# Opening an attention-and-FFN kernel by pairs of heads and 256 tokens, with tanh in the first gelus and a new column order

## The chip, the cores and the metric

One core of one Trainium2 chip. The metric is the device time of one execution, in microseconds (us). Engines: PE (matmul), PEld (weight load, overlapping PE), DVE (VectorE), ACT (ScalarE), POOL (GpSimd, which issues most loads here), SP (SyncE).

## The reference

```python
k_proj = einsum('ks,bhsd->bhkd', E, k);  v_proj = einsum('ks,bhsd->bhkd', F, v)   # 8 x 8 heads, 1024 tokens, D = 64, 64 projected keys
attn = softmax(q @ k_proj^T / 8);  x = attn @ v_proj       # x becomes [8192 tokens, 512]
h = x @ w_in;  g = h * sigmoid(1.702 * h)                  # w_in [512, 2048]
return g @ w_out                                           # float32 [8192, 512]
```

## The kernel before

The 8192 tokens go through in 16 blocks of 512. For each block, `ffn1` makes 16 columns of 128 hidden units (four matmuls and a gelu), `ffn2` multiplies by w_out, and attention work for later blocks is put between the matmuls by `at(block, slot, ...)`. Only block 0 has no earlier block to hide in: its attention stands in the open, and its first FFN runs in two halves of 256 tokens. The parts concerned:

```python
load_kv(k, kt, 0, "k_sb", H // 2)            # two loads
load_kv(q, qt, 0, "q0_sb", H, 0, JB)         # q's first half
load_kv(v, vt, 0, "v_sb", H // 2)            # two loads
for i in range(3): load_w_in(i)              # w_in in 8 pieces of 2 columns each
load_kv(q, qt, 0, "q0_sb", H, JB, JB)        # q's second half
for i in range(3, 8): load_w_in(i)
...
ps_f = ...tile_pool(name="ps_f", bufs=4, space=PSUM)   # one ring of four for k, v, q, scores, ffn1, ffn2, warm-ups
...
for g in range(2):
    k_half(proj0(0, g), g); warm(3)          # warm(n): n matmuls on zeros
for g in (0, 1): q_tr(0, g)()                # q transposed; g = 1 is copied by ScalarE
warm(4)
for u in range(2): scores(0, u)()            # four exps of 512
gelu_table()
for g in range(2):
    v_part(0, proj0(1, g), slice(g, g + 1)); warm(2)
tok(0, 0)(); tok(0, 1)()                     # 128 tokens, all heads: attn @ v, reciprocal, multiply
x_tr(0, 0)(); x_tr(0, 1)()                   # transposes and one 512-wide copy into xT
at(0, 0, tok(0, 2)); at(0, 1, tok(0, 3)); at(0, 4, x_tr(0, 2)); at(0, 6, x_tr(0, 3))
...
for i in range(halves * FC):                 # block 0: half 0's 16 columns, then half 1's
    hf, fc = divmod(i, FC)
    ffn1(j, fc, ...); filled(j, i)
```

The softmax here doesn't subtract the row's maximum and nothing guards it: scores larger than these inputs give would overflow.

## Time and profile before

| | before |
|---|---|
| three executions first seen | 521.7, 521.79, 523.04 us |
| the profiled one | 521.73 us, span 520.0 us |
| first FFN matmul / block 1's first FFN matmul in the chain | 23.79 / 58.44 us |
| PE's granted clock, 23.4 to 26.6 us | 0.50 |

The chain of waits is followed backwards from the last instruction, so it shows what the end hung on. The lines of each view are in the prediction.

### The profile page before, as it was taken

What the parts mean: (1) busy time and instruction counts of PE and PEld (TensorE: products, weight loads), DVE (VectorE), ACT (ScalarE), POOL (GpSimd) and SP (SyncE); (2) the same over time, 40 slices, a digit from 0 to 9 for tenths busy, and PEclk for the clock granted to TensorE, in tenths of its full rate; (3) what the DMA queues carried; (4) which work ended last, traced back from release to release, by engine and by line L of the source; (5) the groups of instructions that cost most, each with busy time, mean ns of one, the idle gap of its engine ahead of it and who ended that gap; (6) DMA issues with size and microseconds to landing.
All of it is one profiled execution on the core that took longest, in us unless ns stands there. A gap on an engine that the chain in (4) does not pass through costs nothing.

```text
span 520.0 us, 6643 instructions
## 1 busy us (share of the span) xinstructions
PE 509.9 (98%) x2830; PEld 233.1 (45%) x2830; DVE 246.6 (47%) x210; ACT 264.4 (51%) x433; POOL 75.7 (15%) x94
## 2 busy tenths in 40 slices
PE   7799999999999999999999999999999999999996
PEld 3485544443444444444444444444444444444442
DVE  2321323674865480827648183664808265560000
ACT  1466355464546547364555645465473646344351
POOL 6354320921510015000420000000000000000000
PEclk9899999999999999999999999999999999999999
DMA  9999999999996019760494301060200101010102
GB/s 169 200 203 185 236 186 160 167 186 156 225 167 162 1 81 153 95 163 0 123 178 119 72 12 76 2 161 2 82 5 1 81 1 81 1 81 2 81 1 81
DMA packets 112750, 53.78 MB, mean 103 GB/s; under 512 B 85584, under 2 KB 110160, under 8 KB 110800
## 3 DMA queue, kind: packets, MB, share of 16 engines
q0 software_dynamic: 83328, 29.37, 49.8%
q1 hardware_dynamic: 29312, 23.73, 16.3%
q8 instruction: 22, 0.36, 0.3%
q10 hardware_dynamic: 80, 0.26, 0.2%
q14 instruction: 8, 0.07, 0.0%
HBM read 59.24 MB, written 16.78 MB: 146 GB/s over the span
## 4 chain that ended last, share of the span: by engine, by line
PE 96%; ACT 1%; DMA 1%; DVE 1%; issue 0%; ACTq 0%
PE f_ps L304 43%; PE f_ps L293 43%; PE f_ps L140 2%; PE f_ps L218 2%; PE d_ps L218 1%; PE n_ps L218 1%; DMA ef_f<-in_E_dram 1%; PE d_ps L264 1%; PE n_ps L279 1%; ACT expT L230 1%; PE f_ps L119 0%; PE f_ps L197 0%; PE f_ps L149 0%; PE f_ps L200 0%; DVE x_sb L270 0%; ACT L234 0%
## 5 line engine op out<-in xcount | busy, mean ns | idle before, releaser
L250 DVE RECIPROCAL rden<-d_ps 128x512 f32<-128x512 f32 x52 | 174.3, 3352 | 149.3 <-PE d_ps L218 149.3
L304 PE MATMUL f_ps<-w_out_sb,gT 128*128 128x512 bf16 x1024 | 230.6, 379 | 0.1
L293 PE MATMUL f_ps<-xT,w_in_sb 128*128 128x512 bf16 (+1 forms) x1088 | 228.4, 368 | 0.7 <-DVE xT L281 0.6
L295 ACT ACTIVATE gT<-f_ps 128x512 bf16<-128x512 f32 (+1 forms) x272 | 155.5, 572 | 89.0 <-PE f_ps L293 87.7
L293 PEld LDWEIGHTS <-w_in_sb 128*128 128x128 bf16 x1088 | 105.4, 98 | 116.9 <-issue 4.9
L304 PEld LDWEIGHTS <-gT 128*128 128x128 bf16 x1024 | 97.2, 98 | 122.4 <-issue 11.3
L307 ACT COPY o_sb<-f_ps 128x512 f32<-128x512 f32 x64 | 37.5, 586 | 138.3 <-PE f_ps L304 128.5
L63 POOL DMA_DIRECT2D q_sb<-in_q_dram x56 | 49.1, 895 | 67.4 <-DMA k_sb<-in_k_dram 28.9
L251 DVE TENSOR_TENSOR xT<-n_ps,rden 128x512 bf16<-128x512 f32 x52 | 36.0, 692 | 5.8 <-DVE rden L250 0.5
L230 ACT ACTIVATE expT<-f_ps 128x512 bf16<-128x512 f32 x64 | 34.8, 600 | 4.7 <-PE f_ps L218 4.7
L57 POOL DMA_DIRECT2D k_sb<-in_k_dram x9 | 7.8, 862 | 107.6 <-PE f_ps L140 105.9
L230 ACT ACT_TABLE_LOAD x13 | 16.7, 1283 | 4.7 <-PE f_ps L218 4.5
L234 ACT ACT_TABLE_LOAD x14 | 18.0, 1283 | 0.2
L269 DVE RECIPROCAL rd<-d_ps 128x4 f32<-128x4 f32 x24 | 4.2, 174 | 22.6 <-PE d_ps L264 22.5
L140 PE MATMUL f_ps<-k_sb,eft 128*64 128x512 bf16 x56 | 13.4, 382 | 0.0
L140 PE MATMUL f_ps<-v_sb,eft 128*64 128x512 bf16 x56 | 13.4, 382 | 0.0
L218 PE MATMUL f_ps<-qT,kt 64*64 64x512 bf16 x128 | 13.2, 399 | 0.1
L204 DVE COPY qT<-f_ps 128x1024 bf16<-128x1024 bf16 x7 | 4.8, 691 | 16.3 <-PE f_ps L200 8.8
L119 PE MATMUL f_ps<-zeros 128*128 128x512 bf16 x30 | 10.1, 480 | 1.2 <-DVE zeros L101 1.2
L270 DVE TENSOR_TENSOR x_sb<-d_ps,rd 128x256 bf16<-128x256 f32 x24 | 10.2, 424 | 0.8
L218 PE MATMUL d_ps<-expT,ones 64*64 64x512 bf16 x104 | 10.2, 382 | 0.0
L218 PE MATMUL n_ps<-expT,vq 64*64 64x512 bf16 x104 | 10.0, 376 | 0.0
(47 smaller groups left out, 99.1 us busy)
## 6 DMA issues: line engine op xcount, KB each, us to landing
out_dram<-o_sb SPq DMA_DIRECT2D x15, 1024.0 KB, 4.5
k_sb<-in_k_dram POOLq DMA_DIRECT2D x7, 1024.0 KB, 15.9
q_sb<-in_q_dram POOLq DMA_DIRECT2D x56, 128.0 KB, 11.3
v_sb<-in_v_dram POOLq DMA_DIRECT2D x7, 1024.0 KB, 10.5
w_in_sb<-in_moe_w_in_dram POOLq DMA_DIRECT2D x8, 256.0 KB, 14.4
w_out_sb<-in_moe_w_out_dram POOLq DMA_DIRECT2D x4, 512.0 KB, 14.1
k_sb<-in_k_dram POOLq DMA_DIRECT2D x2, 512.0 KB, 7.5
q_sb<-in_q_dram POOLq DMA_DIRECT2D x2, 512.0 KB, 13.8
```

The costliest lines, as they stand in the source:

```text
L63: nc.gpsimd.dma_start(out=qt[b][:, j], in_=qv[:, j])
L140: nc.tensor.matmul(kvps[b][r], eft[:, j, e * KP:(e + 1) * KP], (kt, vt)[e][b][:, :, j, :], start=(j == 0), stop=(j == J - 1))
L218: nc.tensor.matmul(outs[i][r], lhsTs[i][ri], rhss[i][ri], start=True, stop=True)
L230: nc.scalar.activation(expT[h][:, 2 * u + i, :], s_ps[i], AF.Exp, scale=scale)
L234: nc.scalar.preload_act_table(AF.Gelu_apprx_sigmoid)
L250: nc.vector.reciprocal(rden, d_ps[i])
L251: nc.vector.tensor_tensor(x_of(h)[:, 2 * u + i, :], n_ps[i], rden, op=ALU.mult)
L270: nc.vector.tensor_tensor(xs[h, t][:, 4 * g:4 * g + 4, :], d_ps[:, :, :D], rd.to_broadcast([P, 4, D]), op=ALU.mult)
L293: nc.tensor.matmul(h_ps, w_in_sb[:, kc, fc * P:(fc + 1) * P], xT[j][:, kc, ts], start=(kc == 0), stop=(kc == KC - 1))
L295: nc.scalar.activation(gts[j][:, fc, ts], h_ps, AF.Gelu_apprx_sigmoid)
L304: nc.tensor.matmul(o_ps[0], gts[j][:, fc, n * P:(n + 1) * P], w_out_sb[:, fc, :], start=(fc == 0), stop=(fc == FC - 1))
L307: nc.scalar.copy(osb[j][:, n, :], o_ps[0])
```

## The change

Its intent: start the FFN earlier by doing only what the first 256 tokens need. q's first quarter is loaded and transposed, the scores and exps are 256 wide, and tok and x_tr go by pairs of heads, so that v's last heads can come later, in small loads. The second 256 tokens' exps come after the FFN has begun. So that they need no switch of ScalarE's table, the first five gelus are made from tanh and two DVE steps. The first FFN's order is changed too: twelve columns for each half, then four. The diff, cut to its core:

```diff
+    load_kv(q, qt, 0, "q0_sb", H, 0, 2)
+    load_kv(v, vt, 0, "v_sb", ((0, 4), (4, 2), (6, 2)))
+    load_kv(q, qt, 0, "q0_sb", H, 2, 2)
+    for i in range(6): load_w_in(i)          # was: 3 pieces, q's second half, 5 pieces
 ...
-            cp = nc.scalar.copy if b == 0 and g == 1 else nc.vector.tensor_copy
-            cp(qT[b][:, 2 * g:2 * g + 2], t_ps)
+            nc.vector.tensor_copy(qT[b][:, 2 * g:2 * g + 2], t_ps)
 ... # v_out: one 64x64 copy per head, ScalarE and DVE in turn (was: two copies of two heads)
 ... # tok(h, p, half), x_tr(h, p, half): a pair of heads and 256 tokens (was: 128 tokens, all heads)
+        if j > 0 or ts.start > 0 or fc > 4:
+            nc.scalar.activation(gts[j][:, fc, ts], h_ps, AF.Gelu_apprx_sigmoid)
+        else:
+            t_sb = work.tile([P, n], F32, name="t_sb", bufs=3)
+            nc.scalar.activation(t_sb, h_ps, AF.Tanh, scale=0.851)
+            nc.vector.tensor_scalar(t_sb, t_sb, 0.5, 0.5, op0=ALU.mult, op1=ALU.add)
+            nc.vector.tensor_tensor(gts[j][:, fc, ts], t_sb, h_ps, op=ALU.mult)
 ...
+    q_tr(0, 0)(); warm(3); scores(0, 0, 0)(); scores(0, 1, 0)()
+    v_out(0, proj0(1, 0, 4), 0, 2); warm(2)
+    tok(0, 0, 0)(); tok(0, 1, 0)(); v_out(0, proj0(1, 4, 2), 2, 1)
+    x_tr(0, 0, 0)(); x_tr(0, 1, 0)(); tok(0, 2, 0)(); v_out(0, proj0(1, 6, 2), 3, 1)
+    x_tr(0, 2, 0)(); tok(0, 3, 0)(); q_tr(0, 1)(); x_tr(0, 3, 0)()
+    order = [(half, fc) for fcs in (range(12), range(12, FC)) for half in range(2) for fc in fcs]
+    at(0, 0, scores(0, 0, 1)); at(0, 1, scores(0, 1, 1)); at(0, 4, gelu_table)
+    for p in range(HP):
+        at(0, 5 + p, tok(0, p, 1)); at(0, 8 + p, x_tr(0, p, 1))
 ... # block 1: load(1) takes v ahead of q, proj(1) four slots earlier; block 0's first FFN2 parts swapped
```

More of the change, by code (lines that the diff above doesn't have):

```diff
@@ L55, in load_kv @@
         sv = src[b].rearrange("h (p j) d -> p h j d", p=P)
-        for h in range(0, H, hs):
-            nc.gpsimd.dma_start(out=dst[b][:, h:h + hs, js:js + jn], in_=sv[:, h:h + hs, js:js + jn])
+        for h, n in [(h, hs) for h in range(0, H, hs)] if isinstance(hs, int) else hs:
+            nc.gpsimd.dma_start(out=dst[b][:, h:h + n, js:js + jn], in_=sv[:, h:h + n, js:js + jn])
     def load_q(b):
@@ L66, in load @@
         load_kv(k, kt, b, "k_sb")
+        if b == 1:
+            load_kv(v, vt, b, "v_sb")
         load_q(b)
-        load_kv(v, vt, b, "v_sb")
+        if b > 1:
+            load_kv(v, vt, b, "v_sb")
     w_in_v = moe_w_in.rearrange("(c p) f -> p c f", p=P)
@@ L81 @@
     make_identity(nc, ident)
-    load_kv(q, qt, 0, "q0_sb", H, 0, JB)
-    load_kv(v, vt, 0, "v_sb", H // 2)
-    for i in range(3):
+    load_kv(q, qt, 0, "q0_sb", H, 0, 2)
+    load_kv(v, vt, 0, "v_sb", ((0, 4), (4, 2), (6, 2)))
+    load_kv(q, qt, 0, "q0_sb", H, 2, 2)
+    for i in range(6):
         load_w_in(i)
     load_kv(q, qt, 0, "q0_sb", H, JB, JB)
-    for i in range(3, 8):
+    for i in range(6, 8):
         load_w_in(i)
@@ L143, in proj, with proj0 @@
         return go
-    def proj0(e, g):
-        ps = f_tile([P, H // 2, D])
-        hs = slice(g * H // 2, (g + 1) * H // 2)
+    def proj0(e, h0, n):
+        ps = f_tile([P, n, D])
         for j in range(J):
-            nc.tensor.matmul(ps, eft[:, j, :], (kt, vt)[e][0][:, hs, j, :],
+            nc.tensor.matmul(ps, eft[:, j, :], (kt, vt)[e][0][:, h0:h0 + n, j, :],
                              start=(j == 0), stop=(j == J - 1))
@@ L164, in k_tr, with v_out @@
         nc.vector.tensor_copy(kts[b % 2][:, p0:p0 + n, :], t_ps)
-    def v_part(b, v_ps, us):
-        vv = v_ps[HI].rearrange("k (u x) d -> k u x d", x=4)
-        for r, xs_, n in ((LO, X_LO, 0), (HI, X_HI, 1)):
-            if b < 2:
-                cp = nc.scalar.copy if b == 0 and n else nc.vector.tensor_copy
-                cp(vxs[b][r].rearrange("k (u x) d -> k u x d", x=4)[:, us, xs_, :D], vv[:, :, xs_, :])
-            if b > 0:
-                nc.vector.tensor_copy(vqs[b % 2][r].rearrange("k (u e) d -> k u e d", e=2)[:, us],
-                                      vv[:, :, xs_, :])
+    def v_out(b, v_ps, p0, n):
+        for i in range(n):
+            p = p0 + i
+            for r, t in ((LO, p % 2), (HI, 1 - p % 2)):
+                if b < 2:
+                    cp = nc.scalar.copy if b == 0 and t == p % 2 else nc.vector.tensor_copy
+                    cp(vxs[b][r, 2 * p + t, :D], v_ps[HI, 2 * i + t, :])
+        if b > 0:
+            vv = v_ps[HI].rearrange("k (u x) d -> k u x d", x=4)
+            for r, xs_ in ((LO, X_LO), (HI, X_HI)):
+                nc.vector.tensor_copy(vqs[b % 2][r].rearrange("k (u e) d -> k u e d", e=2), vv[:, :, xs_, :])
     def kv_out(b):
@@ L182, in go @@
                 nc.sync.dma_start_transpose(out=kts[b % 2], in_=k_b.rearrange("k h d -> k (h d)"))
-            v_part(b, ps, slice(0, 2))
+            v_out(b, ps, 0, HP)
             kbs[b] = k_b
@@ L218, in four, with scores @@
                 nc.tensor.matmul(outs[i][r], lhsTs[i][ri], rhss[i][ri], start=True, stop=True)
-    def scores(h, u):
+    def scores(h, u, half=None):
         b, c = divmod(h, NB2)
+        j0, n = (c * JB, JB) if half is None else (c * JB + half * JB // 2, JB // 2)
+        ts = slice(j0 * P - c * TB, (j0 + n) * P - c * TB)
         def go():
-            if u == 0:
+            if h not in expT:
                 expT[h] = att.tile([P, HP, TB], BF16, name="expT", bufs=3)
-            s_ps = [f_tile([P, TB]) for _ in range(2)]
+            s_ps = [f_tile([P, n * P]) for _ in range(2)]
             four(s_ps, [kts[b % 2][:, 2 * u + i, :] for i in range(2)],
-                 [qT[b][:, c * JB:(c + 1) * JB, 2 * u + i, :] for i in range(2)])
+                 [qT[b][:, j0:j0 + n, 2 * u + i, :] for i in range(2)])
             for i in range(2):
-                nc.scalar.activation(expT[h][:, 2 * u + i, :], s_ps[i], AF.Exp, scale=scale)
+                nc.scalar.activation(expT[h][:, 2 * u + i, ts], s_ps[i], AF.Exp, scale=scale)
         return go
@@ L255, with tok @@
     xs = {}
-    def tok(h, t):
+    def tok(h, p, half):
         def go():
-            xs[h, t] = work.tile([P, H, D], BF16, name="x_sb")
-            for g in range(2):
-                d_ps = ps_d.tile([P, 4, D + 1], F32, name="d_ps")
-                for i in range(2):
-                    p = 2 * g + i
-                    nc.tensor.matmul(d_ps[:, 2 * i:2 * i + 2, :].rearrange("s t d -> s (t d)"),
-                                     expT[h][:, p, t * P:(t + 1) * P],
-                                     vxs[h // NB2][:, 2 * p:2 * p + 2].rearrange("r t d -> r (t d)"),
-                                     start=True, stop=True)
-                rd = work.tile([P, 4, 1], F32, name="rd")
-                nc.vector.reciprocal(rd, d_ps[:, :, D:])
-                nc.vector.tensor_tensor(xs[h, t][:, 4 * g:4 * g + 4, :], d_ps[:, :, :D],
-                                        rd.to_broadcast([P, 4, D]), op=ALU.mult)
+            d_ps = ps_d.tile([P, 4, D + 1], F32, name="d_ps")
+            for i in range(2):
+                t = 2 * half + i
+                nc.tensor.matmul(d_ps[:, 2 * i:2 * i + 2, :].rearrange("s t d -> s (t d)"),
+                                 expT[h][:, p, t * P:(t + 1) * P],
+                                 vxs[h // NB2][:, 2 * p:2 * p + 2].rearrange("r t d -> r (t d)"),
+                                 start=True, stop=True)
+            rd = work.tile([P, 4, 1], F32, name="rd")
+            nc.vector.reciprocal(rd, d_ps[:, :, D:])
+            xs[h, p, half] = work.tile([P, 4, D], BF16, name="x_sb", bufs=4)
+            nc.vector.tensor_tensor(xs[h, p, half], d_ps[:, :, :D], rd.to_broadcast([P, 4, D]), op=ALU.mult)
@@ L272, in tok, with x_tr @@
         return go
-    def x_tr(h, t):
+    def x_tr(h, p, half):
         def go():
-            x_sb = xs.pop((h, t)).rearrange("s h d -> s (h d)")
-            n_ps = ps_n.tile([P, KC, P], BF16, name="n_ps")
-            for c in range(KC):
-                nc.tensor.transpose(n_ps[:, c, :], x_sb[:, c * P:(c + 1) * P], ident)
-            cp = nc.scalar.copy if (h, t) == (0, 0) else nc.vector.tensor_copy
-            cp(x_of(h)[:, :, t * P:(t + 1) * P], n_ps)
+            x_sb = xs.pop((h, p, half)).rearrange("s (i t) d -> s i (t d)", i=2)
+            n_ps = ps_n.tile([P, 2, P], BF16, name="n_ps")
+            for i in range(2):
+                nc.tensor.transpose(n_ps[:, i, :], x_sb[:, i, :], ident)
+            nc.vector.tensor_copy(x_of(h)[:, p, half * TB // 2:(half + 1) * TB // 2],
+                                  n_ps.rearrange("r i s -> r (i s)"))
@@ L294, in ffn1, with ffn2 @@
                              start=(kc == 0), stop=(kc == KC - 1))
-        nc.scalar.activation(gts[j][:, fc, ts], h_ps, AF.Gelu_apprx_sigmoid)
-    def ffn2(j, n, half):
-        b, c = divmod(j, S // TB)
-        if n == 0 and half == 0:
+        if j > 0 or ts.start > 0 or fc > 4:
[5 more added lines that the diff above has]
+            nc.vector.tensor_tensor(gts[j][:, fc, ts], t_sb, h_ps, op=ALU.mult)
+    def ffn2(j, n, fcs):
+        b, c = divmod(j, NB2)
+        if j not in osb:
             osb[j] = work.tile([P, JB, DM], F32, name="o_sb")
-        if half == 0:
-            o_ps[0] = f_tile([P, DM])
-        for fc in range(half * FC // 2, (half + 1) * FC // 2):
-            nc.tensor.matmul(o_ps[0], gts[j][:, fc, n * P:(n + 1) * P], w_out_sb[:, fc, :],
+        if fcs.start == 0:
+            o_ps[n] = f_tile([P, DM])
+        for fc in fcs:
+            nc.tensor.matmul(o_ps[n], gts[j][:, fc, n * P:(n + 1) * P], w_out_sb[:, fc, :],
                              start=(fc == 0), stop=(fc == FC - 1))
-        if half == 1:
-            nc.scalar.copy(osb[j][:, n, :], o_ps[0])
+        if fcs.stop == FC:
+            nc.scalar.copy(osb[j][:, n, :], o_ps.pop(n))
             ov = out[b * S:(b + 1) * S, :].rearrange("(p j) m -> p j m", j=J)
@@ L321 @@
     for g in range(2):
-        k_half(proj0(0, g), g)
+        k_half(proj0(0, 4 * g, 4), g)
         warm(3)
-    for g in (0, 1):
-        q_tr(0, g)()
-    warm(4)
+    q_tr(0, 0)()
+    warm(3)
     for u in range(2):
-        scores(0, u)()
-    gelu_table()
-    for g in range(2):
-        v_part(0, proj0(1, g), slice(g, g + 1))
-        warm(2)
-    tok(0, 0)()
-    tok(0, 1)()
-    x_tr(0, 0)()
-    x_tr(0, 1)()
-    at(0, 0, tok(0, 2))
-    at(0, 1, tok(0, 3))
-    at(0, 4, x_tr(0, 2))
-    at(0, 6, x_tr(0, 3))
-    at(0, 18, q_tr(0, 2))
-    at(0, 20, q_tr(0, 3))
-    at(0, Q, scores(1, 0))
-    at(0, Q + 1, scores(1, 1), gelu_table)
-    for t in range(JB):
-        at(0, Q + 2 + t, tok(1, t))
-        at(0, Q + 3 + t, x_tr(1, t))
+        scores(0, u, 0)()
+    v_out(0, proj0(1, 0, 4), 0, 2)
+    warm(2)
+    tok(0, 0, 0)()
+    tok(0, 1, 0)()
+    v_out(0, proj0(1, 4, 2), 2, 1)
+    x_tr(0, 0, 0)()
+    x_tr(0, 1, 0)()
+    tok(0, 2, 0)()
+    v_out(0, proj0(1, 6, 2), 3, 1)
+    x_tr(0, 2, 0)()
+    tok(0, 3, 0)()
+    q_tr(0, 1)()
+    x_tr(0, 3, 0)()
+    order = [(half, fc) for fcs in (range(12), range(12, FC)) for half in range(2) for fc in fcs]
+    at(0, 0, scores(0, 0, 1))
+    at(0, 1, scores(0, 1, 1))
+    for p in range(HP):
+        at(0, 5 + p, tok(0, p, 1))
+        at(0, 8 + p, x_tr(0, p, 1))
+    at(0, 20, q_tr(0, 2))
+    at(0, 23, q_tr(0, 3))
+    at(0, 4, gelu_table)
+    for u in range(2):
+        at(0, Q + u, scores(1, u))
+    at(0, Q + 1, gelu_table)
+    for p in range(HP):
+        at(0, Q + 2 + p, tok(1, p, 0), tok(1, p, 1))
+        at(0, Q + 3 + p, x_tr(1, p, 0), x_tr(1, p, 1))
+    at(1, 4, proj(1))
+    at(1, 5, kv_out(1))
+    at(1, 7, lambda: k_tr(1, kbs[1], 0), q_dma(2))
     for g in range(4):
-        at(1, 2 + 2 * g, q_tr(1, g))
-    at(1, 8, proj(1))
-    at(1, 9, kv_out(1))
-    at(1, 10, lambda: k_tr(1, kbs[1], 0), q_dma(2))
+        at(1, 8 + 2 * g, q_tr(1, g))
     for u in range(2):
@@ L357 @@
         at(2, O + 3 + u, scores(5, u))
-    for t in range(JB):
-        at(1, O + 2 + t, tok(2, t))
-        at(1, O + 3 + t, x_tr(2, t))
+    for p in range(HP):
+        at(1, O + 2 + p, tok(2, p, 0), tok(2, p, 1))
+        at(1, O + 3 + p, x_tr(2, p, 0), x_tr(2, p, 1))
     at(2, 1, norm(3, 0))
@@ L387 @@
             load(j // NB2 + 2)
-        halves = 2 if j == 0 else 1
-        for i in range(halves * FC):
-            hf, fc = divmod(i, FC)
-            ffn1(j, fc, slice(hf * TB // halves, (hf + 1) * TB // halves))
+        for i, (half, fc) in enumerate(order if j == 0 else [(None, fc) for fc in range(FC)]):
+            ffn1(j, fc, slice(0, TB) if half is None else slice(half * TB // 2, (half + 1) * TB // 2))
             filled(j, i)
-        for s in range(2 * JB):
-            ffn2(j, s // 2, s % 2)
-            filled(j, halves * FC + s)
+        parts = [(n, range(8 * g, 8 * g + 8)) for n in range(JB) for g in range(2)]
+        if j == 0:
+            parts[1:3] = parts[2:0:-1]
+        for s, (n, fcs) in enumerate(parts):
+            ffn2(j, n, fcs)
+            filled(j, (Q if j == 0 else O) + s)
     assert not fill, fill
```

## The prediction

> **What bounds the kernel now.** I read first the busy table of the whole execution, to see which engine has no room:
>
> ```profile
> span 520.0 us, 6643 instructions
> PE 509.9 (98%) x2830; PEld 233.1 (45%) x2830; DVE 246.6 (47%) x210; ACT 264.4 (51%) x433; POOL 75.7 (15%) x94
> ...
> PE   7799999999999999999999999999999999999996
> ...
> PEclk9899999999999999999999999999999999999999
> ```
>
> PE is full everywhere but in the first two slices (13 us each) and the last. "Busy" is not "at its peak", so next the stretch sums, which give pace as well:
>
> ```profile
> core 0: us, PE busy (x) PEld busy (x) DVE busy (x) ACT busy (x) POOL busy (x), PEclk, DMA share, GB/s
> 19.90:23.40 3.50, 1.88 (x17) 0.93 (x15) 2.33 (x9) 1.02 (x4) 1.49 (x3) 0.99 1.45 194
> 23.40:26.60 3.20, 2.81 (x17) 2.01 (x18) 1.59 (x7) 0.77 (x2) 1.24 (x2) 0.50 1.45 196
> ...
> 29.42:41.90 12.48, 12.44 (x133) 10.43 (x132) 1.81 (x3) 9.39 (x25) 5.42 (x7) 1.00 1.27 205
> ```
>
> PE has half its time free from 19.9 to 23.4, and in the 3.2 us after that its granted clock is 0.50. From 29.4 on it is full at clock 1.00. In the chain that ended last, eight 512-column matmuls take 1.73 us piece after piece, 0.216 us each; 64 of them, one half of a block's FFN, are 13.8 us. From 93.7 us on, PE is busy 416.2 of 416.3 us. The diff takes no matmul out of that part, so it can only move the opening: when the first FFN matmul starts (23.79 us), and how long block 0 then takes (block 1 starts at 58.44, so 34.65 us).
>
> The same chain shows what holds the start back:
>
> ```profile
> 13.99 1.03 PE f_ps L197 x32
> ...
> 15.04 1.02 ACT qT L204
> ...
> 16.11 0.46 PE f_ps L218 x4
> 16.57 2.04 ACT expT L230 x4
> ...
> 18.63 1.28 ACT L234
> ...
> 19.93 0.27 ACT vx L171
> ...
> 22.41 0.44 DVE x_sb L270
> ...
> 23.22 0.43 DVE xT L281
> ...
> 23.79 1.01 PE f_ps L293 x4
> ```
>
> q is transposed and ScalarE copies the second half (1.02); four 512-wide exps (2.04); the gelu table (1.28); a v copy that waited behind the table; then four rounds of reciprocal and multiply on DVE at 0.55 us each (20.55 to 22.85); the xT copy; the FFN.
>
> Is the DMA a second bound? The issuing queue waits for old transfers before it issues new ones, and those waits date the landings. In order of issue they read: k's second half 10.9 us, q 13.5, v 16.0 and 18.6, the first three pieces of w_in 19.9, 22.2, 23.4, q's second half 26.1, then w_in 27.4, 28.7, 30.0, 31.4, 32.8. PE in turn first uses w_in's last pieces close to their landing, and waits there once, for 0.32 us:
>
> ```profile
> 32.52 2.08 PEld L293 LDWEIGHTS <-w_in_sb 128*128 128x128 bf16 x20 [0.32 <-DMA w_in_sb<-in_moe_w_in_dram]
> ```
>
> So a merely earlier start would be lost to w_in again. That is why the change also reorders the first FFN: twelve columns for half 0, the same twelve for half 1, then the last four of each.
>
> **What the Trainium skill says.** "ScalarE: Activation LUTs", section "Table sets: the hidden batching unit", lists tanh in the set of exp, and says that only a switch of set costs. So tanh between two sets of exps should need no load. The same page, "What ACT_TABLE_LOAD costs", gives about 1283 ns for a load, and the trace has 1283 ns on average. It also says that back-to-back activations overlap by about 93 ns: here an exp lasts 600 ns and four take 2.06 us, 0.515 each, which agrees.
> "TensorE: Matmul & The Clock Gate", section "Part 1: The HAM clock gate", says that after about 3.4 us with little work the clock drops to half, in a free-running window. The trace agrees: 3.2 us at 0.50, after 3.5 us in which PE was 54% busy. The window's phase is not the kernel's to choose, so I can't tell whether the new kernel will see it.
> "VectorE: DVE Perf Modes", section "The perf-mode tier table", gives fp32 tensor_scalar in SBUF 2x and tensor_tensor, or anything fp32 out of PSUM, 1x. In the trace a 256-wide multiply out of PSUM takes 0.42 us. I estimate the new tensor_scalar on 256 columns at about 0.2 us from the page's rates; no run here shows one yet.
>
> **Part by part.**
> (a) Earlier scores. Only 16 of 32 q transposes stand ahead, and DVE alone copies them (its copy ran from 14.60 to 15.29). The scores start near 15.4 instead of 16.11: -0.7 us.
> (b) Half-width exps. A 256-wide gelu takes 0.383 us here; less the 93 ns overlap that is 0.3 each, so four take some 1.25 us instead of 2.04: -0.8.
> (c) The gelu table leaves the chain: -1.28. In sum, the first d_ps matmul moves from 20.24 to about 17.5. The v pieces (estimated at 205 GB/s from the 10.9 us of k: q quarter 12.2, v 14.8, 16.1, 17.4, second q quarter 18.7, w_in 20.0) come in time for it.
> (d) What is put in ahead of the FFN. The four rounds of reciprocal and multiply stay 2.2 us. But DVE now makes four 256-wide xT copies of 0.29 (the row for kt, 128x256 bf16, shows 0.29) instead of one in the chain: +0.75. Small v copies in its order: +0.3. The copy of the second q quarter, which is in its order before the last xT: +0.69. Hops between PE and DVE, some 0.05 to 0.15 each: the rest. From 17.7 I come to 22.3 for the FFN's start: -1.5 against 23.79.
> (e) Added inside block 0: eight score matmuls of 256 columns (four 512-wide ones are 0.34 us in the chain, so about 0.35 us).
> (f) Five tanh gelus. Each holds its PSUM buffer for tanh 0.38, tensor_scalar 0.2, multiply 0.42 and hops, 1.2 us, in a ring of four that also feeds the scores; PE makes a group in 0.43 us. DVE has 0.65 us for each, 3.3 in all, then four rounds of 0.55 and four copies of 0.29 for half 1: 6.6 us of DVE in a stretch where PE has 12 groups at 0.43 and 1.3 us of other work, 6.5. Writing out the ring by hand I get 8.6 us for this stretch at full clock, so up to 2.1 us of waits. The old kernel lost there only to its clock: 5.63 us for work of 4.3, 1.3 lost. The excess is +0.8 at most by this working; serialised hops in it are pessimistic, so I take +0.5.
> (g) Later in block 0: no wait for w_in, -0.3. The new order of the first FFN2 parts puts another part between the last gelus and their use, and tok by pairs needs only one pair's exps; but the old trace shows no gap there, so 0. proj(1) moves to an earlier slot; v(1) is loaded before q(1), so it should have landed: 0.
> Sum: -1.5 + 0.35 + 0.5 - 0.3 = about -0.95. The pieces ahead of the FFN alone are worth 2.8, of which two thirds are given back.
>
> **Rivals.**
> 1. The gain stands whole: half 1's DVE work hides, no ring wait, no half clock. For it: DVE has no work at all from 29.9 to 35.5 us in the old trace, so its backlog can run out there. Then -1.5 + 0.35 - 0.3 - 1.3 (the cold stretch gone) = -2.7: 519.1 us.
> 2. DVE and the PSUM ring become the bound of the first twelve groups, with the half clock on top. For it: the sum under (f), 6.6 us of DVE in 6.5 of PE. Against: at half clock PE makes a group in 0.86 us, and the DVE then keeps up, so the two losses overlap. Then about +0.5: 522.3.
> 3. Tanh is taken from another table set than exp. With tanh and exps mixed, four or five more loads of 1.28 would come before the fifth column: +5, 527. Against it: the skill's table of sets, and that an author who wrote tanh there for this reason would have looked. 4%.
> 4. The small q pieces (256 B runs at the destination) load slowly. In the old trace the q loads with 128 B runs moved 157 GB/s against 205 to 207 for the others, so 256 KB would take 0.3 us more at the worst; with slack everywhere, nothing at the end.
>
> **Range and chances.** All live outcomes lie within 3 us of 521.8, which is 0.6%. I take 521.0 us (521.79 - 0.95, rounded up a little because the waits in (f) are more likely to be under-counted than the gains). Range 519.4 to 522.4, from rivals 1 and 2. Over 2% either way is 10.4 us; only something outside this list makes that: 1% each. The three runs of before span 521.7 to 523.04, so noise of over a microsecond in one run is to be expected.
>
> **What would show it.** In the new profile: first exps at about 15.7 and 0.3 us apart; no table load between them and the first tanh, one gelu load after the fifth tanh; the first FFN matmul near 22.3; PE waits on DVE's multiply into gT in the first columns; no wait for w_in; block 1's first FFN matmul near 57.5 (58.44 before) and the same length from there. I am wrong in the mechanism if the FFN starts before 21 or after 23.2, if DVE never holds PE in the first twelve groups, or if the part after block 1's start changes by over 0.5 us.

## The result, and the profile after

Six executions of each: before 522.41 us median (521.7 to 523.53), changed 520.7 us median (520.38 to 522.49). A ratio here is the mean time of one kernel's fast runs over that of the other's of the same rounds, so not quite the ratio of the medians: 0.9972, interval 0.9951 to 0.9993. That is 1.5 us, and clear of noise by a little. The six executions of before fall into two groups, 521.7 to 521.79 us and 523.04 to 523.53; against the lower group the changed kernel's median is 1.1 us shorter.

The opening of the changed kernel, from its chain of waits (start us, us, what; lines answering to those of before):

```profile
14.32 0.64 PE f_ps L202 x16
...
15.74 0.35 PE f_ps L222 x4
...
17.58 0.22 ACT vx L175
...
17.82 0.24 DVE vx L175
...
18.09 0.22 ACT vx L175
...
18.33 0.23 DVE vx L175
...
22.38 0.62 DVE qT L208
23.00 0.21 DVE xT L285
```

The 512-wide exps, the gelu table and ScalarE's q copy have left the chain. New in it are four small v copies that alternate between two engines, 1.0 us together with the gaps between them, and DVE's copy of the second q quarter. The next lines of the same chain show what then holds the first columns:

```profile
23.56 0.39 ACT t_sb L305
...
23.97 0.62 DVE t_sb L306
...
24.61 0.43 DVE gT L307
...
25.09 0.61 PE f_ps L298 x4
...
27.91 0.42 DVE gT L307
...
28.45 0.43 DVE x_sb L276
...
31.57 0.30 DVE xT L285
```

From the first tanh (L305, 23.56 us) to 28.89 us DVE is 3.7 of the chain's 5.3 us; from there to half 1's last xT copy the chain is PE's. The stretch sums of the same execution say it in other words (columns as in the prediction):

```profile
20.00:23.40 3.40, 2.68 (x38) 1.71 (x36) 2.95 (x11) 0.21 (x1) 1.18 (x2) 1.00 1.45 197
23.40:26.60 3.20, 2.95 (x27) 2.13 (x27) 2.08 (x6) 2.54 (x9) 2.01 (x4) 1.00 1.45 196
26.60:30.00 3.40, 2.72 (x29) 2.14 (x28) 3.23 (x12) 2.90 (x6) 1.40 (x2) 1.00 1.45 197
```

DVE is 3.23 of 3.40 us busy from 26.6 to 30.0, while PE is 2.72. The clock is 1.00 where before had 0.50.

In this execution (521.62 us, one of the slower of its kernel) E landed 0.39 us later than in that of before: the load took 5.20 us in the chain, not 4.81. It starts block 1 at 58.17 us against 58.44. In a second profile of the same kernel (run 1's, called typical below), an execution of 520.53 us, the first FFN matmul is at 21.90 and block 1 starts at 57.25 us, 1.2 us ahead of before; its whole span is 1.3 us shorter. So everything lies ahead of block 1. One caution about the start: three of the first column's four matmuls now run ahead of the last xT copy, and only the fourth waits for it. In before all four waited until 23.79, so the fourth is what to compare with it: 22.59 us here, 23.25 in the first profile.

```profile
21.90 0.49 PE L298 MATMUL f_ps<-xT,w_in_sb 128*128 128x256 bf16 x3
22.59 0.27 PE L298 MATMUL f_ps<-xT,w_in_sb 128*128 128x256 bf16 x1 [0.20 <-DVE xT L285]
```

### The profile page after: what moved, and what is told of

It is laid out like the page before. It is cut to its first block, busy times and chain, and to the rows that moved or that the text cites. A ratio compares the mean times of both kernels' runs of the same rounds, so it can differ in the third digit from the quotient of the medians.

```text
span 519.8 us, 6658 instructions
## 1 busy us (share of the span) xinstructions
PE 506.2 (97%) x2792; PEld 232.5 (45%) x2843; DVE 253.8 (49%) x242; ACT 263.3 (51%) x437; POOL 77.3 (15%) x96
## 4 chain that ended last, share of the span: by engine, by line
PE 95%; DVE 2%; DMA 1%; ACT 1%; issue 1%; ACTq 0%
PE f_ps L316 43%; PE f_ps L298 42%; PE f_ps L144 2%; PE f_ps L222 2%; PE d_ps L222 1%; PE n_ps L222 1%; DMA ef_f<-in_E_dram 1%; PE f_ps L152 1%; PE f_ps L123 1%; PE n_ps L284 1%; PE d_ps L269 0%; DVE x_sb L276 0%; PE f_ps L205 0%; PE f_ps L202 0%; DVE gT L307 0%
## 5 line engine op out<-in xcount | busy, mean ns | idle before, releaser
L301 ACT ACTIVATE gT<-f_ps 128x512 bf16<-128x512 f32 (+1 forms) x267 | 153.4, 575 | 85.7 <-PE f_ps L298 84.8
L236 ACT ACTIVATE expT<-f_ps 128x512 bf16<-128x512 f32 (+1 forms) x68 | 35.3, 576 | 13.5 <-PE f_ps L222 13.4
L222 PE MATMUL f_ps<-qT,kt 64*64 64x512 bf16 (+1 forms) x136 | 13.8, 386 | 0.0
L274 DVE RECIPROCAL rd<-d_ps 128x4 f32<-128x4 f32 x24 | 4.2, 175 | 15.5 <-PE d_ps L269 15.4
L222 PEld LDWEIGHTS <-kt 64*64 64x64 bf16 x136 | 4.1, 103 | 14.2 <-issue 14.2
```

The lines of the kernel that those rows point to most:

```text
L222: nc.tensor.matmul(outs[i][r], lhsTs[i][ri], rhss[i][ri], start=True, stop=True)
L236: nc.scalar.activation(expT[h][:, 2 * u + i, ts], s_ps[i], AF.Exp, scale=scale)
L301: nc.scalar.activation(gts[j][:, fc, ts], h_ps, AF.Gelu_apprx_sigmoid)
```

## The experiments

Three theories:
- **Chain** (mine): the shorter chain to the first FFN matmul is the gain, reduced by DVE's new work; w_in's landing is a bound that the new order takes away.
- **Clock**: the gain is only that PE no longer falls to half clock at 23.4 us.
- **Parts**: the pairs, the small loads and tanh each carry some of it.

Twelve runs were made in three calls on three chips. The before runs of the calls had medians of 522.46, 522.52 and 521.99 us, so a difference of less than half a microsecond between calls means little; the changed kernel's own medians (520.7, 520.61, 520.65) agree better.

**1. The changed kernel again (no edit).**

> The changed kernel once more, to compare the others with on one chip. It should be 1.0 to 1.8 us faster than the kernel before (ratio 0.9965 to 0.998). In the profile again no half-clock window between 13 and 40 us, first FFN matmul at 22.2 to 22.6, and block 1's first FFN matmul 0.3 to 0.8 us earlier than before's 58.44.

520.61 us median (520.11 to 521.03), ratio 0.9958 (0.9928 to 0.9988). No half clock after 13 us, as expected. The rest came out beyond the ranges named: the ratio, the first FFN matmul at 21.90, and block 1 1.2 us earlier than before's, not 0.3 to 0.8. In the before runs of this call single executions went up to 525.97 us, with a mean clock of 0.989; those with a clock of 0.998 or more took 521.17 to 521.68 us. Part of the mean ratio is those slow executions.

**2. Before, kept warm.**

```diff
     tok(0, 0)()
+    warm(3)
     tok(0, 1)()
     x_tr(0, 0)()
+    warm(2)
     x_tr(0, 1)()
+    warm(2)
```

> The kernel before with seven more warm-up matmuls in PE's gaps between 20 and 23.8 us; nothing else. Clock theory (the gain of the change is only that PE no longer falls to half clock at 23.4 us): 1.3 to 1.6 us faster than before, as fast as the changed kernel. My theory (the last pieces of w_in land at 31.4 and 32.8 us and hold the first half of the FFN whatever the clock): the half-clock window goes, but PE then waits for w_in about 1.2 us instead of 0.3, so only 0.2 to 0.5 us faster.

522.01 us median (521.8 to 522.23), ratio to before 0.9985 (0.9955 to 1.0015). The clock is 1.00 all through, and nothing is won over the undisturbed before runs of the call (521.17 to 521.68 us). Its PEld waits from 13 to 45 us say where the clock's gain went:

```profile
PEld L293 <- DMA w_in_sb<-in_moe_w_in_dram: 1.7, 3, 0.6
```

So does its chain:

```profile
5.78 15.59 DMA w_in_sb<-in_moe_w_in_dram
21.37 0.28 issue
21.66 11.17 DMA w_in_sb<-in_moe_w_in_dram
32.83 0.05 issue
32.87 2.36 PE f_ps L293 x20
```

Followed back from block 1, the chain meets half 0's last matmuls, and these hang on w_in's last piece; nothing of the attention is in it. The clock theory falls: the half-clock window in before's profile was hidden behind the loads. None of the six executions was slow, where five of before's eleven took 522.99 us or more; six are few, and run 11, with the same warm-ups, has one of 522.63.

**3. The changed kernel with gelu throughout.**

```diff
-        if j > 0 or ts.start > 0 or fc > 4:
+        if True:
 ...
-    at(0, 0, scores(0, 0, 1)); at(0, 1, scores(0, 1, 1)); at(0, 4, gelu_table)
+    scores(0, 0, 1)(); scores(0, 1, 1)(); gelu_table()
```

> The changed kernel with gelu for all columns: the second half's scores and exps are put right ahead of the FFN, with the gelu table load behind them, so the first gelu can't run before about 25.7 us. Intent of the change (tanh hides the table load): 1.5 us or more slower than the changed kernel. My theory (tanh's DVE work gives back about what it hides; PE runs four groups ahead in the PSUM ring while the table loads): within 0.6 us of the changed kernel.

521.68 us median (521.1 to 522.4), 1.07 us slower than the changed kernel of the same call. Three of its six executions had a mean clock of 0.995 or 0.996, which none of the changed kernel's had; the three at 0.999 took 521.1 to 521.62 us, 0.5 to 1.0 us slower. By the median of all six both expectations missed; by that of the three (521.16, 0.55 us slower) mine just holds. Its profile fell on a half-clock execution, which lost its time ahead of the first reciprocal (clock 0.61 from 8 to 12 us). From the first reciprocal to block 1 it took 39.11 us (19.85 to 58.96), the changed kernel's typical profile 39.32 (17.93 to 57.25). So the trace shows no gain from tanh behind that point, and where the half microsecond of the full-clock executions lies is open.

**4. Tanh without its DVE steps.**

```diff
-            nc.scalar.activation(t_sb, h_ps, AF.Tanh, scale=0.851)
-            nc.vector.tensor_scalar(t_sb, t_sb, 0.5, 0.5, op0=ALU.mult, op1=ALU.add)
-            nc.vector.tensor_tensor(gts[j][:, fc, ts], t_sb, h_ps, op=ALU.mult)
+            nc.scalar.activation(gts[j][:, fc, ts], h_ps, AF.Tanh, scale=0.851)
```

> Wrong result on purpose: tanh is written to gT and its two DVE steps are left out. If DVE's 6.6 us (tanh steps, then the reciprocals and copies of half 1) is what holds the first twelve groups: 1.0 to 1.8 us faster than the changed kernel, half 1's first group at 29.8 to 30.4 instead of 31.4. If the ring behind the table load on ACT holds them: under 0.4 us faster.

519.53 us median (519.15 to 519.85), 1.1 us faster than the changed kernel; half 1's first group at 29.45 us (30.83 in the changed kernel's profile of the same call), a little ahead of the range named. From the first reciprocal to block 1 it took 38.20 us (17.68 to 55.88), also 1.1 less. Gone is PE's one long wait in the first twelve columns, which the changed kernel's profile lists from 13 to 45 us:

```profile
PEld L269 <- DVE x_sb L276: 0.9, 1, 0.9
```

This is a multiply of half 1 that stands behind tanh's steps in DVE's queue. DVE was the hold, as expected: the two DVE steps of five columns cost 1.1 us of the end. The edit also frees each column's PSUM buffer earlier; the typical profile lists no wait for the multiply into gT, the first profile one of 0.2 us.

**5. Only the order undone.**

```diff
-    order = [(half, fc) for fcs in (range(12), range(12, FC)) for half in range(2) for fc in fcs]
+    order = [(half, fc) for half in range(2) for fc in range(FC)]
```

> The changed kernel with one line undone: the first FFN takes all 16 columns of half 0, then all 16 of half 1. If w_in's last piece (landing near 32.5 to 33 us) is the second bound that the reordering removes: PE waits again for w_in in half 0, up to three times, block 1 starts about 25.9 us after the last piece as with the extra warm-ups, and the kernel is 0.7 to 1.4 us slower than the changed kernel (about as slow as before). If the gain came from the shorter chain alone: within 0.3 us of the changed kernel.

521.98 us median (521.87 to 522.12), ratio to before 0.9989 (0.9974 to 1.0004): no gain over before is left that is clear of noise. In this execution the first FFN matmul came at 21.25 us and the one behind the last xT copy at 21.95, 1.8 us earlier than in before's profile, and it was worth nothing. PEld's waits from 13 to 45 us, and the end of the chain up to 36 us:

```profile
PEld L298 <- DMA w_in_sb<-in_moe_w_in_dram: 2.0, 2, 1.5
```

```profile
20.07 12.62 DMA w_in_sb<-in_moe_w_in_dram
32.69 0.05 issue
32.73 3.23 PE f_ps L298 x28
```

PE arrives early and waits 1.5 us at one piece of w_in. As in run 2, the chain goes back to a load.

**6. The loads undone.**

```diff
-    load_kv(q, qt, 0, "q0_sb", H, 0, 2)
-    load_kv(v, vt, 0, "v_sb", ((0, 4), (4, 2), (6, 2)))
-    load_kv(q, qt, 0, "q0_sb", H, 2, 2)
+    load_kv(q, qt, 0, "q0_sb", H, 0, JB)
+    load_kv(v, vt, 0, "v_sb", H // 2)
```

> The changed kernel with the opening's loads as before: q's first half in one piece ahead of v, v in two halves. v's halves land at about 16.0 and 18.6 us, the changed kernel's PE wants them at 16.5 and 18.7. If the loads were not what held the chain: within 0.3 us of the changed kernel. If q quarter and v's small pieces carry the gain: 0.8 us or more slower.

521.3 us median (520.95 to 522.1), ratio to before 0.9978 (0.9963 to 0.9993). That is 0.65 to 0.7 us slower than the changed kernel in the calls to either side, between the two expectations; without a yardstick in this call I call it some half microsecond. PEld waits for v 1.3 us in all, 1.0 of it once:

```profile
PEld L151 <- DMA v_sb<-in_v_dram: 1.3, 2, 1.0
```

**7. Two tanh columns instead of five.**

```diff
-        if j > 0 or ts.start > 0 or fc > 4:
+        if j > 0 or ts.start > 0 or fc > 1:
 ...
-    at(0, 4, gelu_table)
+    at(0, 1, gelu_table)
```

> The changed kernel with tanh for two columns (those issued before the second exps) instead of five, and the gelu table loaded right behind those exps. DVE has 2.1 us less to do in the first twelve groups (three times 0.28 + 0.42). If DVE's queue holds those groups, as the run without the DVE steps showed (1.1 us): 0.6 to 1.1 us faster than the changed kernel, with the right result. If the table load, now in front of three more groups, takes its place: within 0.3 us.

520.23 us median, in two groups: four executions of 519.97 to 520.37 us at a clock of 0.999 or more, two of 521.87 and 522.2 at 0.997. The four are about 0.5 us below the changed kernel, just short of what was expected. The profile fell on one of the two, but from the first reciprocal to block 1 it took 38.68 us (20.08 to 58.76), 0.6 less than the changed kernel's. It shows DVE idle for 1.29 us while the gelu table loads: part of what tanh occupied is now unused.

**8. The second q quarter copied by ScalarE, two steps earlier.**

```diff
+            cp = nc.scalar.copy if b == 0 and g == 1 else nc.vector.tensor_copy
+            cp(qT[b][:, 2 * g:2 * g + 2], t_ps)
 ...
+    q_tr(0, 1)()
     x_tr(0, 2, 0)()
     tok(0, 3, 0)()
-    q_tr(0, 1)()
```

> The changed kernel with the second q quarter's transposes issued two steps earlier and copied by ScalarE, which is idle there, so that DVE's 0.69 us copy no longer stands before the last xT copy. If that copy is on the chain (0.62 us of it in the trace): 0.3 to 0.7 us faster, first tanh 0.6 us nearer to the first reciprocal. If DVE's queue behind it just takes over: under 0.2 us.

520.76 us median (520.43 to 521.14), no gain. The copy left the chain, and the first tanh was 4.92 us after the first reciprocal (22.75 less 17.83), not 4.97. In the changed kernel PE's last transposes ran beneath DVE's q copy; now DVE's last multiply, these transposes (0.30 us) and the xT copy (0.30) stand one after the other. A wait in the chain of 0.62 us was worth nothing, because another stood just behind it.

**9. The changed kernel as yardstick of the third call (no edit).**

> The changed kernel, as the yardstick on this chip: 520.3 to 520.8 us, with single runs up to 522 when E lands late and PE falls to half clock before k's projection.

520.65 us median (520.49 to 522.63), ratio 0.9971 (0.9958 to 0.9984). The profile fell on its slowest execution: the clock from 8 to 12 us averages 0.60, after a stretch (4 to 8 us) with PE busy 1.52 of 4.00 us, and k's projection starts at 10.54 us, not 8.58 as in the typical profile. The profiles of runs 3 and 7 show the same (0.61 and 0.57).

```profile
4.00:8.00 4.00, 1.52 (x7) 0.47 (x5) 0.69 (x1) 1.90 (x2) 4.00 (x6) 0.97 1.12 169
8.00:12.00 4.00, 3.89 (x20) 2.26 (x20) 0.77 (x2) 0.00 (x0) 1.50 (x3) 0.60 1.43 192
```

E's load took 5.19 us in this chain. It took 5.20 in the first profile of the changed kernel, whose clock stayed at 1.00 from 8 to 12 us, after PE had been busy 2.41 of 4.00 us. So a late E alone is not enough.

**10. Before with only the order changed.**

```diff
-    for i in range(3): load_w_in(i)
+    for i in range(6): load_w_in(i)
     load_kv(q, qt, 0, "q0_sb", H, JB, JB)
-    for i in range(3, 8): load_w_in(i)
+    for i in range(6, 8): load_w_in(i)
 ...
-            hf, fc = divmod(i, FC)
+            hf, fc = order[i]                 # twelve columns of each half, then four
```

> The kernel before with only the order of the first FFN (twelve columns of each half, then the last four of each) and six pieces of w_in ahead of q's second half. If w_in was the second bound that hid everything else: the half-clock window at 23.4 us (1.5 us) is now paid in full, no wait for w_in is left, and the kernel is 0.5 to 1.2 us faster than before, 521.2 to 521.9. If the order is only worth something together with the shorter chain: within 0.3 us of before.

521.42 us median, from 520.32 to 523.04, ratio to before 0.999 (0.9972 to 1.0007). The spread follows the clock: 520.32 and 520.42 at 0.998 and 1.0, 521.23 and 521.61 at 0.996 and 0.995, 522.99 and 523.04 at 0.993 and 0.992. That reads as if half clock were paid for now that the loads are out of the way; no slow execution of it was profiled, so this is not shown. At a clock of 0.998 or more this small edit is as fast as the changed kernel. It moves both the columns and q's second half behind six pieces of w_in, and does not tell the two apart; run 5 undid the columns alone.

**11. The same, kept warm** (the edits of runs 10 and 2 together).

> The same with the seven warm-up matmuls in PE's gaps between 20 and 23.8 us: the old, longer chain (FFN from 23.6), full clock, no w_in wait, and no tanh steps on DVE. By the sums: twelve groups with their tok and transposes to about 29.8, FFN2 at about 39.6 against 40.7 of the changed kernel, so 519.5 us, 0.7 to 1.4 us faster than the changed kernel. If pairs of heads, small loads and tanh carry the gain: slower than the changed kernel by 0.5 us or more.

520.8 us median (four of six from 520.69 to 520.85; 521.72 and 522.63 the others), ratio to before 0.9982 (0.9969 to 0.9996). Its chain, and what PE had in the stretch that was the trouble:

```profile
23.84 0.60 PE f_ps L293 x4
...
28.76 5.24 PE f_ps L293 x48
```

```profile
26.60:30.00 3.40, 3.40 (x37) 3.09 (x36) 1.13 (x3) 2.63 (x7) 1.63 (x2) 1.00 1.45 197
30.00:34.00 4.00, 4.00 (x39) 3.41 (x39) 0.00 (x0) 3.50 (x10) 2.14 (x3) 1.00 1.32 204
```

The FFN starts at 23.84 us, as late as before, but PE is full from 26.6 on, with DVE at a third until 30.0; no wait for w_in is listed. It falls 1.3 us short of my 519.5 and equals the changed kernel (520.65). So neither expectation held in size. What it shows is plain: the reordering of run 10, with warm-ups, gets to within 0.15 us of what the whole change gets, less than these runs can tell apart.

**12. The best of it.**

```diff
     # runs 7 and 8 together, and
-        at(0, 5 + p, tok(0, p, 1)); at(0, 8 + p, x_tr(0, p, 1))
+        at(0, 2 + p, tok(0, p, 1)); at(0, 5 + p, x_tr(0, p, 1))
-    warm(12)
+    warm(14)
```

> The changed kernel with two tanh columns, the second q quarter copied by ScalarE, half 1's tok three slots earlier (while the gelu table loads and DVE is idle), and two more warm-ups ahead of E's landing. Each of the first two frees DVE; the third uses the freed time. 519.0 to 519.7 us, and fewer slow executions. If the table load takes DVE's place as the hold: no better than two tanh columns alone, 520.0.

519.73 us median (519.37 to 520.47), ratio to before 0.9954 (0.9943 to 0.9966), correct; 0.9 us faster than the changed kernel of the same call, and faster than both kernels. The 519.73 is just above the range I gave. Half 1's tok now fills DVE's idle time behind the table load:

```profile
23.40:26.60 3.20, 3.04 (x32) 2.56 (x33) 2.89 (x11) 3.17 (x9) 1.58 (x3) 1.00 1.45 196
26.60:30.00 3.40, 3.40 (x36) 3.09 (x35) 1.49 (x6) 2.64 (x8) 1.62 (x2) 1.00 1.45 197
```

From 26.6 to 30.0 us PE is full (2.72 of 3.40 in the changed kernel). None of its five executions was slow; five are too few to credit the two more warm-ups.

## Why the prediction was right or wrong

The number was right: 521.0 us predicted, 520.7 measured, in the range. The predicted gain was 0.8 to 0.95 us; block 1 starts 1.2 us earlier in the typical profile, and the ratio's 1.5 us has before's slow executions in it. Of the steps behind it:

- **(a), (b), (c), what leaves the chain: right.** In the typical profile the scores start at 15.08 us (15.4 named) and the first exp at 15.42 (15.7), the four exps took 1.21 us (1.25), and no table load stands between exps and tanh. The first d_ps matmul (exps times v) is at 17.45 us (17.5 named).
- **(d), the FFN's start: nearly right in sum, wrong in a term.** The matmul behind the last xT copy came at 22.59 us in the typical profile and at 23.25 in the first, against 22.3. The "Small v copies in its order: +0.3" took 1.0 us in the chain ahead of the first reciprocal alone, because ScalarE and DVE take turns. "PSUM — Partial Sum Buffer" of the Trainium skill, section "PSUM bank collisions raise a hardware error", says that two engines on the same 32 partitions of one bank at once, two readers too, is an error, and that the compiler's scheduler puts a dependency between them. I had not looked it up. The trace agrees in so far as the copies at 17.58, 17.82, 18.09 and 18.33 never overlap and each of the last three is released by the other engine's; that the bank is the reason is not shown.
- **(f), DVE's hold on the first twelve groups: right, the place of the wait wrong.** By hand 8.6 us were found; from the FFN's start as above to half 1's first group it is 8.24 us in the typical profile (22.59 to 30.83) and 8.66 in the first (23.25 to 31.91). The DVE steps are 1.1 us of it (run 4). But PE waits for half 1's multiply into x_sb, the attention's result (0.9 us, run 4), not for the one into gT, the gelu's. The tensor_scalar took 0.29 us, not 0.2: I had left out the fixed part in the skill's table ("VectorE: DVE Perf Modes", section "The perf-mode tier table": 1227 ns for 2048 elements, where an estimate from the rate alone is 1067). And the "work of 4.3" is too high: the chain's 28 FFN matmuls and 16 others between 23.79 and 29.42 us come to 3.95 at the full-clock pace of the same chain, so before lost 1.7 us there, not 1.3, and "+0.5" was rather too much than too little.
- **(g), "no wait for w_in, -0.3": right as a difference of the two traces, wrong as a price.** It was read from PE's only wait of 0.32 us. But a PE slowed by half clock arrives late at w_in and waits little; speeded up, it waits 1.7 us (run 2) or 2.0 (run 5). So the 1.3 us that (f) counts as lost to the clock can't be won without the new order either. Undoing the order alone costs 1.3 us (521.98 against 520.65, in two calls), as much as the whole gain. What I wrote about it in words, that an earlier start would be lost to w_in again, is what run 5 shows; the prices of the parts did not follow the words.
- **Rival 1's "-1.3 (the cold stretch gone)"** was worth nothing in the kernel before (run 2), since the loads hid it.

From the FFN's start to block 1 it was 34.65 us before, 34.66 in the typical profile and 34.92 in the first, where (e) to (g) add 0.55. So by the typical profile (d) promised some 0.3 us too much, and block 0 gave back some 0.3 to 0.5 less than reckoned; that these two nearly cancel is luck.

The sentence "The pieces ahead of the FFN alone are worth 2.8, of which two thirds are given back" was too kind: together, pairs, small loads and tanh bring about 0.15 us over the reordering with warm-ups (520.65 against 520.8), within noise. They start the FFN 1.25 us earlier than in run 11 (22.59 against 23.84), but from there to block 1 the changed kernel takes 34.66 us and run 11 33.72 (to 57.56). What they win ahead of the FFN they lose behind it, and run 4 puts 1.1 us of that on tanh's DVE steps. Taking out the loads singly cost about half a microsecond (run 6); for tanh this is open (run 3).

Not settled: what makes single executions slow (522.49 and 522.63 us of the changed kernel). In run 9's profile it is half clock ahead of k's projection, after PE had stood waiting for E; a late E alone does not do it, and whether the phase of the clock's window does is open. The kernel before has slow executions at full clock too (523.05 us at 1.0 in the third call), of which there is no profile. Nor was it tested what the swapped FFN2 parts and the earlier proj(1) do; behind block 1's start nothing changed.

## What to carry to other kernels

Before you shorten a chain, ask what bounds the stage if the chain were free. A wait of 0.3 us at a load, in an engine that is running slow for another reason, can be a bound that is merely being met just in time. Filling the slack with harmless work (run 2) is a cheap test of this. And when work moves to an engine off the path, add up that engine's queue for the stretch in which you put it, not for the whole execution: DVE, 47% busy overall in the kernel before, came to be 3.7 of 5.3 us of the chain.

## What the Trainium skill lacked or had wrong

- "TensorE: Matmul & The Clock Gate", section "Part 1: The HAM clock gate", lets the clock drop after an idle window. In the runs it drops after windows in which PE is far from idle, and not always: PE was busy 1.81 of 3.40 us from 20.0 to 23.4 in the profile of before and went to 0.50; in run 10's profile it was busy 1.78 of the same 3.40 us and stayed at 1.00, though where its windows began is not known. The page gives no share of busy time at which it drops.
- The same page counts the ramp's cost as under 1% of a typical span. It says nothing of where half clock costs nothing at all: 3.2 us at 0.50 in the profile of before, with executions at full clock hardly faster (521.53 us at a mean clock of 0.995, 521.17 to 521.68 at 0.998 or more, in the first call), since a load was the bound (run 2).
